# A fused attention and gated MLP kernel: two weight reads and the steps that follow them, put at other places in round 2

## The chip, the core and the metric

The kernel runs on one core of a Trainium2 chip. The metric is the time of one execution in device microseconds, the median of several runs. Lower is better.

## What is computed

Eight batches of 448 tokens go through an attention with 12 heads of 64 and a sigmoid in the softmax's place, and then through a gated MLP whose gate is mixed over the tokens:

```python
scores = q @ k.T / sqrt(64) - log(448)
x = concat_heads(sigmoid(scores) @ v)            # 8 x 448 x 768
h = relu(x @ w_in)                               # w_in: 768 x 1024
u, v = h[..., :512], h[..., 512:]
v_n = (v - mean(v)) / sqrt(var(v) + 1e-6)
v_s = w_spatial @ v_n + b_spatial[:, None]       # over tokens
out = (u * v_s) @ w_out                          # w_out: 512 x 768
```

Everything is float32. The large products are made from high and low parts of their operands: a copy rounded for TensorE (the high part) and the rest (the low part), with three products per pair.

## The kernel before, in words

**Rounds.** A round (`m`, 0 to 3; the text counts them 1 to 4) takes two batches through attention and then through the MLP. In rounds 2 to 4 the MLP's products follow Strassen's scheme: an operand is cut into four blocks, and seven products of blocks and of sums of blocks take the place of eight (`by_blocks`, operand names such as "11", "s2", "t3"). The weights need sums of blocks for that, and x needs such sums as well.

**Where the weights' sums come from.** In round 1 the joined values of w_in's two halves are written to DRAM, `w_full["g"]` for the gate half and `w_full["u"]` for the other. `weight_sums(kind, w)` (L522) is called twice at the start of round 2 (L1565, L1566). It issues one DMA that reads the whole values back into SBUF (L525, 1,536 KB), and appends a generator of eight steps to the list `jobs`. Steps 1 to 4 make one sum of blocks each on VectorE (L543, L546, L549, L552) and, one step later, ScalarE casts the sum to its high part (L535). Steps 5 to 8 are the finishing passes: VectorE subtracts the high part for the low one (L539), and SyncE writes both to DRAM (L540). From there `load_block` (L508) reads the blocks back for the products. `wholes(m)` (L579) is a third job: two steps that add x's high and low parts to whole values for the sums of x (L584).

**Who runs the jobs.** `spare(n)` (L478) takes n steps from the list, in its order, wherever it is called. The instructions of each engine run in the order in which the program issues them (`in_program_order`), and SyncE issues all DMAs of this stretch, so the place of a call in the code sets the place on every engine's queue.

**Attention by fours.** `attention_by_fours(m)` (L1311) takes the 12 units of a round (a unit is a batch and two heads) in three groups of four. For a group, `n` is its first unit. The loads of the next units' q and k (`raw`, L308) are issued at its start (L1337) and after its first splits (L1361). Then come 12 score tiles on TensorE (L378): VectorE copies four of them out of PSUM (L1354), ScalarE puts the others through the sigmoid (L342). VectorE splits the next units' operands into high and low parts (`attention_splits`, L321 and L328). The value products (L1382) fill two accumulators, `pavs[0]` and `pavs[1]`. After a part of them come `late` (a table of functions by group), `spare` and `split_values` (L131 on ScalarE, L132 on VectorE), which empties `pavs[0]`; `pavs[1]` is emptied by a copy on ScalarE (L1484 after the first group, L1480 after the second). The next group's short scores (L360, the tail of 64 tokens) and their sigmoids stand between.

**PSUM.** All of these tiles share one pool of four buffers of two banks (`ps_2`). They go round: the first score tile of a group takes the buffer of `pavs[0]`, the second that of `pavs[1]`, the third and fourth those of the two short tiles, the fifth that of the first.

The calls in question, at the end of a group that another one follows:

```python
for f in late.pop(n - first, ()):
    f()
spare(8 if n + 4 == end else 3 if n > first else 6)
...
    split_values(pavs[0], *units[n])
if n + 4 < end:
    spare(1)
```

So the two jobs of eight steps are run in pieces of 6 and 1 (first group), 3 and 1 (second group) and 8 (third group, with the two steps of `wholes`). After the last group `values_by_blocks` (L589) makes the sums of x (L628 and the lines behind it) and starts the gate products (`vx`, L1016).

Of the kernel before, what the change touches and what calls it, by code (L numbers as in the profile page):

```python
# [14 lines left out]
P = 128  # L15
# [20 lines left out]
def attn_gmlp_kernel(  # L36
# [485 lines left out]
    def weight_sums(kind, w):  # L522

        w7, order = KINDS[kind]
        nc.sync.dma_start(w[:, 1].bitcast(F32), w_full[kind])  # L525

        def both(name):
            at = NAMES.index(name) * BLOCK
            return w[:, :, at : at + BLOCK]

        def whole(name):
            return both(name)[:, 1].bitcast(F32)

        def cast(name):
            nc.scalar.copy(both(name)[:, 0], whole(name))  # L535

        def finish(name, of):
            hi, lo = (both(name)[:, a] for a in range(2))
            nc.vector.tensor_sub(lo, whole(name), hi.bitcast(F32))  # L539
            nc.sync.dma_start(w7[order.index(of)], both(name).bitcast(F32))  # L540

        def steps():
            nc.vector.tensor_add(whole("22"), whole("21"), whole("22"))  # L543
            yield True
            cast("22")
            nc.vector.tensor_sub(whole("21"), whole("11"), whole("21"))  # L546
            yield True
            cast("21")
            nc.vector.tensor_sub(whole("11"), whole("22"), whole("11"))  # L549
            yield True  # L550
            cast("11")
            nc.vector.tensor_sub(whole("12"), whole("12"), whole("11"))  # L552
            yield True
            cast("12")
            finish("22", "s1")
            yield True
            finish("21", "s3")
            yield True
            finish("11", "s2")
            yield True  # L560
            finish("12", "s4")
            yield True

        jobs.append(steps())

    def high_of_sum(name):
        nc.scalar.copy(staged[name][:, 0], whole[name])
# [726 lines left out]
    def ahead(f, n, end=len(units)):  # L1294
        if n < end:
            f(*units[n])

    def start_loads(m):
# [6 lines left out]
        if not m:  # L1305
            ahead(attention_loads, n + 3)

    late = {}
    early = {}

    def attention_by_fours(m):  # L1311
# [18 lines left out]
        for n in range(first, end, 4):  # L1330
# [4 lines left out]
                short_scores(n + 2)  # L1335
            for i in range(3):
                ahead(attention_loads, n + 4 + i, end)  # L1337
            ats, pending = {}, []
            for i, t in full:
                unit = units[n + i // 2 * 2]  # L1340
# [77 lines left out]
            if not m:  # L1418
                sigmoid(ats[by_vector[2]], ats[by_vector[2]])
                for pair in range(2):  # L1420
                    order = sorted(full[6 * pair : 6 * pair + 6], key=lambda at: at in by_vector)
                    for i, t in order:
                        value_products(
                            pavs[pair],
                            *units[n + 2 * pair],
                            t + i % 2 * (NFULL + 1),
                            ats[i, t],
                            start=i not in begun,
                        )
                        begun.add(i)  # L1430
                    if pair == 0:
                        last_scores()
                        load_weights(7 if n + 4 < end else 9)
                        for i2 in range(3):
                            ahead(attention_splits, n + 4 + i2, end)
                for pair in range(2):
                    unit = units[n + 2 * pair]
                    value_products(pavs[pair], *unit, NFULL, shorts[n + 2 * pair], start=False)
                split_values(pavs[0], *units[n])
                ahead(value_loads, n + 4, end)  # L1440
            else:
                one, two = firsts
                value_steps(0, one[:2])
                value_steps(1, two[:1])
                leave(0, value_steps(0, one[2:]))
                value_steps(1, two[1:2])
                leave(0, value_steps(0, one, swapped=True))
                last_scores()
                ahead(attention_splits, n + 6, end)
                for f in late.pop(n - first, ()):  # L1450
                    f()
                spare(8 if n + 4 == end else 3 if n > first else 6)
                value_steps(1, two[2:3])
                if n + 4 == end:
                    leave(1, value_steps(1, two[3:]))
                value_steps(0, [(NFULL, NFULL)])
                if n + 4 == end and m:
                    whole = whole_x["tile"]
                    x, odd = x_of(*units[n])[:, :, 1], pavs[0][:, 1, :S]
                    nc.scalar.copy(whole[:, 2, 2], pavs[0][:, 0, :S])  # L1460
                    nc.scalar.copy(x[:, 0], odd)
                    nc.vector.tensor_sub(whole[:, 3, 0], odd, whole[:, 2, 0])
                    nc.vector.tensor_sub(x[:, 1], odd, x[:, 0].bitcast(F32))
                else:
                    split_values(pavs[0], *units[n])
                if n + 4 < end:
                    spare(1)
                ahead(value_loads, n + 4, end)
                if n + 4 < end:
                    leave(1, value_steps(1, two[3:]))  # L1470
                    short_scores(n + 4)
                value_steps(1, firsts[1][1:], swapped=True)
# [71 lines left out]
    for m in range(B // 2):  # L1544
        ring = []
        if m:
            whole_x["tile"] = const.tile([P, 4, KH, S], F32, tag="w_out", name=f"whole_{m}")
            early.update(
                (i, whole_x["tile"][:, 2 + i].rearrange("p k s -> p (k s)")[:, : 2 * S])
                for i in range(2)  # L1550
            )

            def gate_ring():
                ring.append(gate_region(f"w_g7_{m}")[:, GAP : GAP + 8 * BLOCK])
                w_g.append(ring[0])
                for pos in range(HELD):
                    load_block("g", ORDER_1, pos)

            def up_ring(ps):
                for pos in ps:  # L1560
                    load_block("u", ORDER_V, pos)

            if m == 1:
                sums_of = gate_region("w_g_sums")[:, : 8 * BLOCK]
                weight_sums("g", sums_of.rearrange("p (a c) -> p a c", a=2))  # L1565
                weight_sums("u", const.tile([P, 2, NCC * F], F32R, tag="w_u", name="w_u_sums"))  # L1566
            else:
                w_u.append(const.tile([P, 2, NCC * F], F32R, tag="w_u", name=f"w_u_{m}"))
                late[0] = [lambda: up_ring(range(2))]
                late[4] = [lambda: up_ring(range(2, HELD))]  # L1570
            late[8] = [lambda: jobs.append(wholes(m)), gate_ring]
        attention(m)
        slots_of_mlp(m)
        b0, b1 = 2 * m, 2 * m + 1
# [92 lines left out]
```

## Time and profile before

| what | value |
|---|---|
| median of 3 runs | 641.74 us (640.69 to 644.13) |
| the profiled execution | 641.68 us |
| its span, first to last instruction | 638.8 us |
| TensorE busy with products | 624.8 us, 98% |
| VectorE busy | 453.8 us, 71% |
| ScalarE busy | 341.3 us, 53% |
| GpSimd busy | 20.8 us, 3% |
| mean granted clock of TensorE | 0.993 of full speed |
| HBM traffic over the span | 217 GB/s |

The span is 2.9 us shorter than the execution's time; this rest lies outside the instructions. Busy shares are means over stages with different limits. The chain of waits follows the execution back from its last instruction, at each step to what released it; what stands in it set the end.

### The profile page before, as it was taken

What the parts mean: (1) busy time and instruction counts of PE and PEld (TensorE: products, weight loads), DVE (VectorE), ACT (ScalarE), POOL (GpSimd) and SP (SyncE); (2) the same over time, 40 slices, a digit from 0 to 9 for tenths busy, and PEclk for the clock granted to TensorE, in tenths of its full rate; (3) what the DMA queues carried; (4) which work ended last, traced back from release to release, by engine and by line L of the source; (5) the groups of instructions that cost most, each with busy time, mean ns of one, the idle gap of its engine ahead of it and who ended that gap; (6) DMA issues with size and microseconds to landing.
All of it is one profiled execution on the core that took longest, in us unless ns stands there. A gap on an engine that the chain in (4) does not pass through costs nothing.

```text
span 638.8 us, 10383 instructions
## 1 busy us (share of the span) xinstructions
PE 624.8 (98%) x4136; PEld 488.4 (76%) x4136; DVE 453.8 (71%) x635; ACT 341.3 (53%) x444; POOL 20.8 (3%) x63
## 2 busy tenths in 40 slices
PE   9999999999978989999999999999999999999997
PEld 3646789999826649999985667999996655999996
DVE  4989789999758868277775757638788555835773
ACT  6987322345658853173457785137247776516443
POOL 0000001000000000010000000002000000002000
PEclk9999999999998999999999999999999999999999
DMA  8774754279948768691575662487169554559044
GB/s 298 266 228 143 225 149 140 71 308 355 342 180 324 294 257 327 175 392 70 191 266 211 242 246 97 123 284 310 33 225 350 196 184 169 168 135 392 30 152 169
DMA packets 59632, 139.22 MB, mean 218 GB/s; under 512 B 15680, under 2 KB 31552, under 8 KB 59328
## 3 DMA queue, kind: packets, MB, share of 16 engines
q1 hardware_dynamic: 59152, 138.22, 61.9%
q8 instruction: 32, 0.52, 0.3%
q10 hardware_dynamic: 432, 0.34, 0.2%
q14 instruction: 16, 0.13, 0.1%
HBM read 102.37 MB, written 36.18 MB: 217 GB/s over the span
## 4 chain that ended last, share of the span: by engine, by line
PE 91%; DVE 3%; DMA 3%; ACT 1%; issue 1%; SPq 0%; ACTq 0%; DVEq 0%
PE o L1016 16%; PE psc L378 13%; PE pav L1382 12%; PE pg L950 10%; PE vx L1016 7%; PE ux L1016 7%; PE uy L1016 5%; PE pav L427 5%; PE pv L460 5%; PE pu L460 5%; PE vy L1016 3%; DMA raw<-qk_dram 3%; PE psc L360 3%; ACT xs L619 1%; PE pg L925 1%
## 5 line engine op out<-in xcount | busy, mean ns | idle before, releaser
L342 ACT ACTIVATE ats<-psc,bias_s 128x896 f32<-128x896 f32 x102 | 95.2, 1008 | 22.2 <-PE pav L1382 13.5
L378 PE MATMUL psc<-qks 64*128 64x448 f32 x840 | 90.0, 369 | 6.0 <-DVE x_s L132 6.0
L378 PEld LDWEIGHTS psc<-qks 64*128 64x128 f32 x840 | 79.1, 188 | 21.0 <-DVE x_s L132 7.7
L1382 PE MATMUL pav<-ats,v 64*64 64x448 f32 x720 | 76.0, 539 | 0.0
L1016 PE MATMUL o<-x_s,w_out 128*128 128x448 f32 x324 | 65.8, 362 | 0.0
L950 PE MATMUL pg<-w_sp_s,mlp 128*128 128x448 f32 x320 | 65.8, 364 | 0.0
L1016 PEld LDWEIGHTS o<-x_s,w_out 128*128 128x128 f32 x324 | 60.6, 188 | 4.3
L950 PEld LDWEIGHTS pg<-w_sp_s,mlp 128*128 128x128 f32 x320 | 59.7, 188 | 5.2 <-issue 1.2
L1382 PEld LDWEIGHTS pav<-ats,v 64*64 64x64 f32 x720 | 28.2, 132 | 37.4 <-issue 26.3
L328 DVE TENSOR_TENSOR qks<-raw,qks 128x848 fp32r<-128x848 f32 x46 | 47.4, 1040 | 1.1
L1016 PE MATMUL vx<-x_s,w_g 128*128 128x448 f32 x216 | 45.3, 365 | 2.6 <-ACT vr L676 2.5
L1016 PEld LDWEIGHTS vx<-x_s,w_g 128*128 128x128 f32 x216 | 40.0, 188 | 8.4 <-ACT vr L676 3.7
L1016 PE MATMUL ux<-x_s,w_u 128*128 128x448 f32 x162 | 33.9, 362 | 0.0
L1016 PEld LDWEIGHTS ux<-x_s,w_u 128*128 128x128 f32 x162 | 30.4, 188 | 2.0
L321 DVE CAST qks<-raw 128x848 fp32r<-128x848 f32 x38 | 22.7, 597 | 10.1 <-DMA raw<-qk_dram 7.9
L460 PE MATMUL pu<-x_s,w_u_s 128*128 128x448 f32 x144 | 29.0, 362 | 0.0
L460 PE MATMUL pv<-w_g_s,x_s 128*128 128x512 f32 x126 | 28.9, 391 | 0.0
L460 PEld LDWEIGHTS pu<-x_s,w_u_s 128*128 128x128 f32 x144 | 27.0, 188 | 1.8
L460 PEld LDWEIGHTS pv<-w_g_s,x_s 128*128 128x128 f32 x126 | 23.6, 188 | 5.6 <-PE pav L427 0.7
L1085 ACT CAST x_s<-g 128x896 fp32r<-128x896 f32 x11 | 10.4, 944 | 32.1 <-DVE g L1082 32.1
L427 PE MATMUL pav<-ats,v 128*64 128x448 f32 (+1 forms) x144 | 27.1, 545 | 0.0
L1170 DVE TENSOR_TENSOR us<-uy,us 128x448 f32<-128x448 f32 x6 | 3.7, 621 | 32.6 <-ACT us L1169 32.6
(205 smaller groups left out, 1022.9 us busy)
## 6 DMA issues: line engine op xcount, KB each, us to landing
raw<-qk_dram SPq DMA_DIRECT2D x47, 456.0 KB, 6.1
w_g<-w_g SPq DMA_DIRECT2D x21, 768.0 KB, 6.8
w_u<-w_u SPq DMA_DIRECT2D x21, 768.0 KB, 6.7
w_out<-w_out SPq DMA_DIRECT2D x21, 768.0 KB, 10.0
v<-v_dram SPq DMA_DIRECT2D x24, 448.0 KB, 4.3
wraw<-w_in_dram SPq DMA_DIRECT2D x12, 512.0 KB, 5.0
v<-vt SPq DMA_DIRECT2D x48, 112.0 KB, 2.5
wraw<-w_out_dram SPq DMA_DIRECT2D x6, 512.0 KB, 4.2
```

What stands on the lines that cost most here:

```text
L321: (nc.vector.tensor_copy if b > 1 or halfway else nc.scalar.copy)(s[:, 0], raw)
L328: nc.vector.tensor_sub(s[:, 1], loaded[b, hp][:, HALF:], s[:, 0].bitcast(F32))
L342: nc.scalar.activation(at, src, AF.Sigmoid, bias=bias_s, scale=QK)
L360: nc.tensor.matmul(psc[odd * HALF : (odd + 1) * HALF, j, :S], raw[rows, :HALF], raw[rows, HALF + Q :], start=True, stop=True,)
L378: nc.tensor.matmul(psc[:, j, :S], st[rows, k : k + P], mv[rows, Q:PART], start=i == 0, stop=i == len(ops) - 1,)
L427: nc.tensor.matmul(pav[heads, odd, :S], vt[rows, t, heads], at[rows, j], start=start, stop=t == NFULL,)
L460: nc.tensor.matmul(ps, st, mv, start=i == 0, stop=i == len(ops) - 1)
L619: nc.scalar.copy(t[:, 0], src[:, ks])
L950: nc.tensor.matmul(pg[:, i, :S], st, mv, start=n == 0 and not ended, stop=n == len(ops) - 1 and ended,)
L1016: nc.tensor.matmul(out_ps, stationary(w, i, k)[:, a], moving[mv][k][c], start=(to, i) not in started and n == 0, stop=n == len(ops) - 1, s ...
L1085: nc.scalar.copy(homes[name][0][:, i], src[:, i])
L1382: ins = nc.tensor.matmul(pavs[pair][heads, i % 2, :S], vt[rows, t if t == NFULL else t + i % 2 * (NFULL + 1), heads], at[rows, j], start=i ...
```

## The change

`weight_sums` no longer issues its DMA itself but returns a function that does. For w_g that function is put into a new table, `soon`, and is called in the first group of round 2 behind the three unit loads at the group's start; for w_u it goes into `late` and is called after the splits of that group, behind the fourth unit load. The pieces of the jobs become 5 and 2 in the first group and 4 and 2 in the second, where they were 6 and 1, and 3 and 1; so 13 of the 16 steps, and no longer 11, stand ahead of the third group. There, `wholes` is put at the head of the list, ahead of the steps that are left of w_u's. The other rounds have no other job in the list at that point.

```diff
@@ -522,7 +522,9 @@
     def weight_sums(kind, w):
 
         w7, order = KINDS[kind]
-        nc.sync.dma_start(w[:, 1].bitcast(F32), w_full[kind])
+
+        def load():
+            nc.sync.dma_start(w[:, 1].bitcast(F32), w_full[kind])
 
         def both(name):
             at = NAMES.index(name) * BLOCK
@@ -562,6 +564,7 @@
             yield True
 
         jobs.append(steps())
+        return load
 
     def high_of_sum(name):
         nc.scalar.copy(staged[name][:, 0], whole[name])
@@ -1305,6 +1308,7 @@
         if not m:
             ahead(attention_loads, n + 3)
 
+    soon = {}
     late = {}
     early = {}
 
@@ -1335,6 +1339,8 @@
                 short_scores(n + 2)
             for i in range(3):
                 ahead(attention_loads, n + 4 + i, end)
+            for f in soon.pop(n - first, ()):
+                f()
             ats, pending = {}, []
             for i, t in full:
                 unit = units[n + i // 2 * 2]
@@ -1449,7 +1455,7 @@
                 ahead(attention_splits, n + 6, end)
                 for f in late.pop(n - first, ()):
                     f()
-                spare(8 if n + 4 == end else 3 if n > first else 6)
+                spare(8 if n + 4 == end else 4 if n > first else 5)
                 value_steps(1, two[2:3])
                 if n + 4 == end:
                     leave(1, value_steps(1, two[3:]))
@@ -1464,7 +1470,7 @@
                 else:
                     split_values(pavs[0], *units[n])
                 if n + 4 < end:
-                    spare(1)
+                    spare(2)
                 ahead(value_loads, n + 4, end)
                 if n + 4 < end:
                     leave(1, value_steps(1, two[3:]))
@@ -1562,13 +1568,14 @@
 
             if m == 1:
                 sums_of = gate_region("w_g_sums")[:, : 8 * BLOCK]
-                weight_sums("g", sums_of.rearrange("p (a c) -> p a c", a=2))
-                weight_sums("u", const.tile([P, 2, NCC * F], F32R, tag="w_u", name="w_u_sums"))
+                soon[0] = [weight_sums("g", sums_of.rearrange("p (a c) -> p a c", a=2))]
+                sums_of = const.tile([P, 2, NCC * F], F32R, tag="w_u", name="w_u_sums")
+                late[0] = [weight_sums("u", sums_of)]
             else:
                 w_u.append(const.tile([P, 2, NCC * F], F32R, tag="w_u", name=f"w_u_{m}"))
                 late[0] = [lambda: up_ring(range(2))]
                 late[4] = [lambda: up_ring(range(2, HELD))]
-            late[8] = [lambda: jobs.append(wholes(m)), gate_ring]
+            late[8] = [lambda: jobs.insert(0, wholes(m)), gate_ring]
         attention(m)
         slots_of_mlp(m)
         b0, b1 = 2 * m, 2 * m + 1
```

SyncE's queue at the start of round 2, before (`v` and `raw` are loads of a unit's values and of its q and k, the first number in a name is the head pair):

```order
L313 DMA v_2_1488<-v_dram 128x896
L525 DMA w_g_sums<-w_full_g 128x3072
L525 DMA w_u_sums<-w_full_u 128x3072
L308 DMA raw_4_1508<-qk_dram 128x912
L308 DMA raw_5_1510<-qk_dram 128x912
L308 DMA raw_0_1512<-qk_dram 128x912
L308 DMA raw_1_1550<-qk_dram 128x912
L540 DMA w_g<-w_g_sums 256x1x768 x3
L313 DMA v_4_1689<-v_dram 128x896
L313 DMA v_0_1715<-v_dram 128x896
L308 DMA raw_2_1726<-qk_dram 128x912
```

and with the change:

```order
L313 DMA v_2_1488<-v_dram 128x896
L308 DMA raw_4_1506<-qk_dram 128x912
L308 DMA raw_5_1508<-qk_dram 128x912
L308 DMA raw_0_1510<-qk_dram 128x912
L527 DMA w_g_sums<-w_full_g 128x3072
L308 DMA raw_1_1549<-qk_dram 128x912
L527 DMA w_u_sums<-w_full_u 128x3072
L542 DMA w_g<-w_g_sums 256x1x768 x3
L313 DMA v_4_1689<-v_dram 128x896
L313 DMA v_0_1715<-v_dram 128x896
L308 DMA raw_2_1726<-qk_dram 128x912
```

The three loads ahead of L308's fourth now precede both weight reads, and w_u's read follows the fourth load; from the writes of w_g's results on the order is as it was.

VectorE between the first and the second group, from the sums of w_g to the copy of the second group's first score tile, before:

```order
L543 TENSOR_TENSOR w_g_sums<-w_g_sums 128x768
L546 TENSOR_TENSOR w_g_sums<-w_g_sums 128x768
L549 TENSOR_TENSOR w_g_sums<-w_g_sums 128x768
L552 TENSOR_TENSOR w_g_sums<-w_g_sums 128x768
L539 TENSOR_TENSOR w_g_sums<-w_g_sums 128x768 x2
L132 TENSOR_TENSOR x_s<-pav_0_1624,x_s 128x2x448
L539 TENSOR_TENSOR w_g_sums<-w_g_sums 128x768
L1485 CAST x_s<-ats_1495 128x2x448
L1354 COPY wval_s<-psc_4_0_1732 128x896
```

and with the change:

```order
L545 TENSOR_TENSOR w_g_sums<-w_g_sums 128x768
L548 TENSOR_TENSOR w_g_sums<-w_g_sums 128x768
L551 TENSOR_TENSOR w_g_sums<-w_g_sums 128x768
L554 TENSOR_TENSOR w_g_sums<-w_g_sums 128x768
L541 TENSOR_TENSOR w_g_sums<-w_g_sums 128x768
L132 TENSOR_TENSOR x_s<-pav_0_1623,x_s 128x2x448
L541 TENSOR_TENSOR w_g_sums<-w_g_sums 128x768 x2
L1491 CAST x_s<-ats_1493 128x2x448
L1360 COPY wval_s<-psc_4_0_1732 128x896
```

One finishing pass has gone from ahead of L132, which empties the first accumulator, to behind it, where there are now two.

VectorE at the same place between the second and third group, before:

```order
L539 TENSOR_TENSOR w_g_sums<-w_g_sums 128x768
L543 TENSOR_TENSOR w_u_sums<-w_u_sums 128x768
L546 TENSOR_TENSOR w_u_sums<-w_u_sums 128x768
L132 TENSOR_TENSOR x_s<-pav_0_1843,x_s 128x2x448
L549 TENSOR_TENSOR w_u_sums<-w_u_sums 128x768
L1354 COPY wval_s<-psc_2_0_1937 128x896
```

and with the change:

```order
L541 TENSOR_TENSOR w_g_sums<-w_g_sums 128x768
L545 TENSOR_TENSOR w_u_sums<-w_u_sums 128x768
L548 TENSOR_TENSOR w_u_sums<-w_u_sums 128x768
L551 TENSOR_TENSOR w_u_sums<-w_u_sums 128x768
L132 TENSOR_TENSOR x_s<-pav_0_1843,x_s 128x2x448
L554 TENSOR_TENSOR w_u_sums<-w_u_sums 128x768
L541 TENSOR_TENSOR w_u_sums<-w_u_sums 128x768
L1360 COPY wval_s<-psc_2_0_1942 128x896
```

ScalarE there, before:

```order
L535 CAST w_u_sums<-w_u_sums 128x768
L131 CAST x_s<-pav_0_1843 128x2x448
L535 CAST w_u_sums<-w_u_sums 128x768
L342 ACTIVATE at_2_3_1908<-psc_2_3_1909,bias_s 128x2x448
L1480 COPY whole_1490<-pav_1_1844 128x896
L342 ACTIVATE at_4_3_1930<-psc_4_3_1931,bias_s 128x2x448
L342 ACTIVATE ats_1495<-psc_2_1_1945,bias_s 128x896
```

and with the change:

```order
L537 CAST w_u_sums<-w_u_sums 128x768 x2
L131 CAST x_s<-pav_0_1843 128x2x448
L537 CAST w_u_sums<-w_u_sums 128x768 x2
L342 ACTIVATE at_2_3_1913<-psc_2_3_1914,bias_s 128x2x448
L1486 COPY whole_1490<-pav_1_1844 128x896
L342 ACTIVATE at_4_3_1935<-psc_4_3_1936,bias_s 128x2x448
L342 ACTIVATE ats_1493<-psc_2_1_1950,bias_s 128x896
```

A third sum of w_u stands ahead of L132 on VectorE, the fourth sum and a finishing pass behind it; on ScalarE two casts instead of one stand ahead of L131 and two instead of one behind it, ahead of the short scores' sigmoid and of the copy that empties the second accumulator.

## Rows read from the trace of the kernel before

**Rows 1.** Chain of waits, rounds 2 and 3: start us, us, what.

```profile
166.14 1.73 PE psc L360 x16
...
168.79 13.05 DMA raw<-qk_dram
...
231.23 3.02 DVE whole L584 x2
...
239.04 3.88 PE vx L1016 x18
...
328.86 1.80 PE psc L360 x16
...
350.28 7.42 PE psc L378 x72
...
377.31 10.75 PE pav L1382 x112
...
388.08 1.10 DVE whole L628
...
391.91 3.87 PE vx L1016 x18
```

**Rows 2.** Timeline of TensorE: start us, us, instruction, [idle before <-releaser].

```profile
193.41 9.00 PE L378 MATMUL psc<-qks 64*128 64x448 f32 x72 [5.99 <-DVE x_s L132]
...
239.04 1.28 PE L1016 MATMUL vx<-x_s,w_g 128*128 128x448 f32 x5 [2.47 <-ACT vr L676]
```

**Rows 3.** Timeline of SyncE's queue, round 2: DMA issues.

```profile
167.81 0.41 SPq L525 DMA_DIRECT2D w_g_sums<-w_full_g  x1
168.28 0.42 SPq L525 DMA_DIRECT2D w_u_sums<-w_full_u  x1
...
168.79 4.09 SPq L308 DMA_DIRECT2D raw<-qk_dram  x4
...
191.46 3.35 SPq L540 DMA_DIRECT2D w_g<-w_g_sums  x3
```

**Rows 4.** DMA issues, by kind: count, KB each, us from issue to landing.

```profile
w_g_sums<-w_full_g SPq DMA_DIRECT2D x1, 1536.0 KB, 9.2
...
raw<-qk_dram SPq DMA_DIRECT2D x1, 456.0 KB, 12.6
```

**Rows 5.** Windows: busy us of each engine, granted clock, DMA share, GB/s.

```profile
176.00:182.00 6.00, 6.00 (x71) 2.55 (x67) 0.14 (x1) 4.43 (x5) 0.20 (x2) 1.00 0.99 412
...
190.00:192.00 2.00, 0.00 (x0) 0.00 (x0) 2.00 (x3) 1.84 (x3) 0.00 (x0) 0.50 0.00 0
...
238.00:240.00 2.00, 0.96 (x5) 0.90 (x6) 1.97 (x3) 1.43 (x4) 0.00 (x0) 1.00 0.96 375
```

**Rows 6.** Timeline of VectorE and ScalarE between the first and second group of round 2.

```profile
181.86 0.60 DVE L321 CAST qks<-raw 128x848 fp32r<-128x848 f32 x1 [6.70 <-DMA raw<-qk_dram]
...
186.63 0.95 DVE L543 TENSOR_TENSOR w_g_sums<-w_g_sums 128x768 f32<-128x768 f32 x1
...
191.34 0.90 ACT L131 CAST x_s<-pav 128x896 fp32r<-128x896 f32 x1
...
192.27 1.09 DVE L132 TENSOR_TENSOR x_s<-pav,x_s 128x896 fp32r<-128x896 f32 x1
...
193.28 0.95 DVE L539 TENSOR_TENSOR w_g_sums<-w_g_sums 128x768 fp32r<-128x768 f32 x1
```

**Rows 7.** Timeline of VectorE and ScalarE between the second and third group of round 2.

```profile
204.13 0.60 DVE L321 CAST qks<-raw 128x848 fp32r<-128x848 f32 x1 [1.24 <-DMA raw<-qk_dram]
...
207.94 1.04 DVE L328 TENSOR_TENSOR qks<-raw,qks 128x848 fp32r<-128x848 f32 x1
...
212.28 0.83 ACT L535 CAST w_u_sums<-w_u_sums 128x768 fp32r<-128x768 f32 x1
...
213.02 1.01 ACT L342 ACTIVATE at<-psc,bias_s 128x896 f32<-128x896 f32 x1
...
213.92 0.91 ACT L1480 COPY whole<-pav 128x896 f32<-128x896 f32 x1
```

## Prediction

> **What bounds the kernel now.** I began with the busy shares: TensorE is busy for 98% of the span, so only its gaps can be won, or time at a lower clock. Then I compared the rounds in the chain of waits. Round 2 runs from its first score products at 166.14 us to 239.04, where the gate products' second operand starts: 72.9 us. Round 3 does the same work from 328.86 to 391.91, 63.05 us [rows 1]. So round 2 has about 9.8 us that its neighbour hasn't.
>
> The timeline of TensorE says where. It stands still for 5.99 us before 193.41, and the 72 score products then take 9.00 us [rows 2] instead of 7.42 [rows 1], 1.58 more: the granted clock is 0.50, its lower level of 1.2 GHz, from the idle stretch on [rows 5]. At the end of the round it waits 2.47 us more before 239.04 [rows 2]. That makes 10.0 us; the rest of the round is 0.2 us quicker than round 3.
>
> The cause is upstream. SyncE issues w_g's and w_u's whole values at 167.81 and 168.28 and the next units' loads only then [rows 3]. The first of these is 13.05 us on its way [rows 1]; VectorE has sat idle for 6.70 us when it lands at 181.84 [rows 6]. Three splits later, at 186.63, the sums of w_g start; L132, which frees the first bank that TensorE wants, stands behind them and runs from 192.27, and TensorE goes on at 193.41 [rows 2, 6]. At the round's end the whole values of x (L584) run at 231.23 [rows 1], behind w_u's finishing passes; in round 3 the step that follows (L628) starts 0.02 us after the last value product, at 377.31 + 10.75 = 388.06 [rows 1].
>
> **The loads.** The queue keeps its bytes, and its order changes: three unit loads of 456 KB go ahead of w_g's 1,536 KB, the fourth stands between w_g and w_u. At the 412 GB/s of this stretch [rows 5] the first load loses 3.1 MB in front of it, 7.6 us, and lands at 174.2, before VectorE wants it (181.86 - 6.70 = 175.16) [rows 6]. w_g landed at 167.81 + 9.2 = 177.0 [rows 3, 4]; 1.40 MB ahead of it cost 3.4 us: 180.4. VectorE's three splits end at 175.16 + 3 x 1.6 = 180.0. So the sums start at **T = 180.4** instead of 186.63. The fourth load and w_u wait on nothing new: the fourth keeps its wait for a buffer, and the queue has drained by about 172.44 + 12.6 = 185.0 in either order [rows 4], long before w_u's sums are begun.
>
> **First to second group.** From T to TensorE's start I take 193.41 - 186.63 = 6.78 us as it is [rows 2, 6]: L131 on ScalarE, which stands behind the four casts of w_g there, ends at 192.24 and sets L132's 192.27 [rows 6], so one finishing pass fewer ahead of L132 gives nothing. T + 6.78 = 187.2, and TensorE is free at 193.41 - 5.99 = 187.42. The gap goes, and with it the fall of the clock. Two finishing passes of 0.95 us instead of one [rows 6] now stand between L132 and the copy that frees the bank for the fifth score tile: some 0.6 us for TensorE, which the next part covers.
>
> **What is late next.** The third write of w_g's results is issued when the last of these passes ends: T + (192.27 + 1.09 - 186.63) + 2 x 0.93 = T + 8.6 = 189.0, where it was 193.28 + 0.95 = 194.23 [rows 6]. Behind it SyncE's queue holds two value loads and then the loads of the third group's units, the first of which VectorE got at 204.13, after waiting 1.24 us for it [rows 7]. From the last pass to that landing it was 9.9 us with the engines full; the bytes ahead are the same, so it lands at 198.9. VectorE would be ready at 195.9: before it was 204.13 - 1.24 = 202.89, 9.5 us after TensorE's start, of which 1.58 were the slow clock, and I add the 0.6. **The DMA queue sets this group**, though TensorE's own work would let it go on at 187.4 + 0.6 + 19.6 = 207.6 (350.28 back to 328.86, less the first 1.80 us of shorts [rows 1], is 19.6 per group).
>
> **Second to third group.** Three splits end 208.98 - 204.13 = 4.85 us after the landing [rows 7], at S = 203.75. Now three steps of w_u instead of two stand ahead of L132, and two instead of one behind it, with two casts on ScalarE. From S on: the last pass of w_g and three sums of about 0.95 us each (S + 3.75); ScalarE's second cast ends at S + 3.6, L131 takes 0.90 and L132 1.09: S + 5.5, and TensorE may start. Then the fourth sum to S + 6.4, and the fourth cast, which waits for it, 0.83 to S + 7.25. Behind that cast on ScalarE stand the sigmoid of the short scores (1.01, S + 8.2) and the copy of the second accumulator, L1480 (0.91) [durations from rows 6, 7]. That copy frees the bank of the second score tile: **S + 9.0 = 212.75**. Before, L1480 ended at 213.92 + 0.91 = 214.83 [rows 7], before TensorE needed it. The new wait is about 3 us long; VectorE's own extra pass ends at S + 7.25 and is covered by it. From below this wait can cost nothing, if S comes early; the bound above is these 3 us and what S slips.
>
> The write of w_u's first result now stands ahead of the third group's two value loads on SyncE's queue, issued at S + 7.25 = 211.0. Those values are wanted at 219.5. The third write of w_g, with two such loads and one more load behind, took 9.9 us in all; one write less should bring them in time, and the worst is some 1.4 us, kept for the range.
>
> **The end of the round.** Eleven score tiles of 7.42 / 12 us, 10.75 us of value products and the 3.85 us from 388.06 to 391.91 [rows 1] follow: 212.75 + 6.8 + 10.75 + 3.85 = 234.15. The whole values run straight behind VectorE's last copies, ahead of the three finishing passes that are left, and both end more than 4 us before the last product: the 2.47 us go. w_u's blocks are read back no later than before. Nothing changes on PE or POOL, nor in the other rounds, where the list of jobs is otherwise empty.
>
> **Sum.** 239.04 - 234.15 = 4.9 us of the 9.8 are won: 6.0 + 1.6 + 2.5 at the three places, less some 5 at the two waits that come instead. The profiled execution took 641.68 us, 0.06 below the median of the runs shown: 641.7 - 4.9 = **636.8 us**. What can be told from no change is about 0.5%, 3.2 us: below 638.5 is faster, above 644.9 slower.
>
> **The rivals.**
> - *All comes back.* If the third group's loads land when VectorE is ready, S = 195.9 + 4.85 = 200.75, 3.0 us sooner: 633.8. If ScalarE's copy isn't waited for either, round 2 ends as round 3 does, 391.91 - 350.28 = 41.63 us after 187.4, at 229.0: 631.7. For it speaks that the second group's neighbour in round 3 has no such wait; against it, that VectorE waited 1.24 us already with a TensorE at half clock [rows 5, 7]. Chance 0.20.
> - *The clock falls at the new wait.* The gap of 5.99 us brought the granted clock to 0.50, that of 2.47 left it at 1.00 [rows 2, 5]; 3 us lie between, nearer to the second. If it falls, the third group's scores take the 9.00 us once more: 636.8 + 1.6 = 638.4. Chance 0.10. [...]
> - *w_g's values come too late.* If the DMA engines shared their time among the reads under way, w_g's would end with w_u's, at 185.0 or later. The end of the round is T + 53.75, so from T = 185.3 on nothing is won; at the old 186.63 the second pass behind L132 makes it 1.35 us worse: 643.0, slower than before. Against it: the small load behind the two big ones landed 4.8 us after w_g did (181.84 against 177.0), in the order of issue [rows 1, 4]. Chance 0.03. The Trainium skill (DMA: Bandwidth & Descriptors, Queues, rings and completion order) says that each engine takes the descriptors of one queue in ring order, though completion is not strictly first in, first out; by that rule this rival is out.
> - *Part of it.* T or the third group's loads slip by 1.7 us to 4.9 us, through the value loads or a slower drain: 638.5 to 641.7. Chance 0.12.
>
> **How the numbers follow.** The forecast has the remaining 0.55, its own range 635.2 to 638.4. 8 times in 10 the time should lie between 633.6 and 639.4: this leaves out the full return to 631.7 (0.05), most of the partial case (0.10) and the late values (0.03). Faster by over 0.5%: 0.54 + 0.20 + half of the clock's 0.10 and a little of the partial case, 0.81. Same: 0.17. Slower: 0.02.
>
> **What would show it.** Right: no idle of TensorE before the second group and its scores in about 8 us at full clock; w_g landing near 180.4; VectorE waiting for the third group's first load; a wait of some 3 us before the second score tile of the third group, released by L1480's copy; no wait at the second gate operand beyond round 3's. It is wrong if TensorE still stands over 1 us before the second group (T was late), or if the third group begins without a wait (the queue was sooner than I say).

## The result and the profile after

The changed kernel takes 635.89 us (median of 6 runs, 635.44 to 636.25), the kernel before 641.93 us (6 runs). The ratio is 0.990, 95% interval 0.987 to 0.993: 6.0 us faster, where 4.9 was forecast. In the profiled executions the span falls from 638.8 to 634.0 us, by 4.8, and the time from 641.68 to 635.77, by 5.9: the other microsecond lies outside the instructions, 2.9 us before and 1.8 with the change. One execution is not the median. The spans of the kernel before, in its runs beside the experiments below, lie between 637.3 and 642.4 us, and in the eleven profiles that follow round 2 starts anywhere from 165.43 to 166.91 us, ahead of every edit. So a single profile places a wait well and a total only to within some 2 us.

The chain of waits of the changed kernel, round 2 (start us, us, what):

```profile
165.77 1.67 PE psc L360 x16
...
168.97 10.92 DMA w_g_sums<-w_full_g
...
191.50 6.24 DMA raw<-qk_dram
...
210.84 1.67 PE psc L378 x12
...
212.55 7.26 PE psc L378 x48
219.81 10.76 PE pav L1388 x112
...
230.59 1.10 DVE whole L631
...
234.42 3.87 PE vx L1019 x18
```

The round starts at 165.77 and reaches the gate products' second operand at 234.42: 68.65 us, where it was 72.9 before and 63.05 in round 3 [rows 1]. So 4.25 us of the 9.8 came back and some 5.6 are still there. Of the 4.8 us of span, 0.37 stand ahead of round 2, where nothing was changed. The chain runs through w_g's read, then through the third group's first load at 191.50, then through the start of the third group.

TensorE's timeline shows the rest (start us, us, instruction, [idle before <-releaser]):

```profile
187.01 2.68 PE L378 MATMUL psc<-qks 64*128 64x448 f32 x24
189.97 5.08 PE L378 MATMUL psc<-qks 64*128 64x448 f32 x48 [0.28 <-DVE wval_s L1360]
195.63 1.74 PE L1388 MATMUL pav<-ats,v 64*64 64x448 f32 x16 [0.58 <-ACT wval_s L342]
...
208.20 0.88 PE L378 MATMUL psc<-qks 64*128 64x448 f32 x6 [0.32 <-DVE x_s L132]
210.84 8.97 PE L378 MATMUL psc<-qks 64*128 64x448 f32 x66 [1.76 <-ACT at L342]
```

The idle stretch of 5.99 us ahead of the second group [rows 2] is gone: its scores start at 187.01 without a wait. Two small waits follow, 0.28 and 0.58 us. The third group is where the time is lost now: its first score tile starts at 208.20, its second only at 210.84 after 1.76 us of idle, and the rest of its scores take 8.97 us instead of about 6.8. The windows say why these are slow (busy us of each engine, granted clock, DMA share, GB/s):

```profile
208.00:210.00 2.00, 0.88 (x6) 0.48 (x6) 2.00 (x4) 0.95 (x2) 0.00 (x0) 1.00 0.00 0
...
214.00:216.00 2.00, 2.00 (x14) 1.76 (x14) 1.99 (x2) 1.16 (x2) 0.00 (x0) 0.50 1.03 416
```

The clock is at 1.00 while TensorE waits and at 0.50, its lower level, for a while behind it. VectorE's timeline answers to [rows 6] and [rows 7]:

```profile
174.72 0.59 DVE L321 CAST qks<-raw 128x848 fp32r<-128x848 f32 x1
...
179.91 0.96 DVE L545 TENSOR_TENSOR w_g_sums<-w_g_sums 128x768 f32<-128x768 f32 x1 [0.34 <-DMA w_g_sums<-w_full_g]
...
185.55 1.09 DVE L132 TENSOR_TENSOR x_s<-pav,x_s 128x896 fp32r<-128x896 f32 x1 [0.84 <-ACT x_s L131]
186.56 1.82 DVE L541 TENSOR_TENSOR w_g_sums<-w_g_sums 128x768 fp32r<-128x768 f32 x2
...
197.76 0.60 DVE L321 CAST qks<-raw 128x848 fp32r<-128x848 f32 x1 [2.20 <-DMA raw<-qk_dram]
...
201.58 1.04 DVE L328 TENSOR_TENSOR qks<-raw,qks 128x848 fp32r<-128x848 f32 x1
...
208.07 0.95 DVE L554 TENSOR_TENSOR w_u_sums<-w_u_sums 128x768 f32<-128x768 f32 x1
...
219.66 3.02 DVE L587 TENSOR_TENSOR whole<-x_s 128x1344 f32<-128x1344 f32 x2
222.59 2.69 DVE L541 TENSOR_TENSOR w_u_sums<-w_u_sums 128x768 fp32r<-128x768 f32 x3
...
230.59 1.09 DVE L631 TENSOR_TENSOR whole<-pav,whole 128x896 f32<-128x896 f32 x1
```

VectorE no longer waits for the next units' load: the splits start at 174.72, straight behind the last copy. It waits 0.34 us for w_g (179.91) and 2.20 us for the third group's first load (197.76). From there it works without a gap to L132 but for ScalarE's casts. x's whole values (L587) run at 219.66, and L631 starts with the last value product; the 2.47 us of idle at the round's end are gone. ScalarE at the boundary to the third group:

```profile
209.05 0.83 ACT L537 CAST w_u_sums<-w_u_sums 128x768 fp32r<-128x768 f32 x1 [1.29 <-DVE w_u_sums L554]
209.79 1.00 ACT L342 ACTIVATE at<-psc,bias_s 128x896 f32<-128x896 f32 x1
210.69 0.90 ACT L1486 COPY whole<-pav 128x896 f32<-128x896 f32 x1
211.47 1.02 ACT L342 ACTIVATE at<-psc,bias_s 128x896 f32<-128x896 f32 x1
```

The cast at 209.05 has waited 1.29 us for w_u's fourth sum on VectorE (L554, 208.07). The short scores' sigmoid stands behind it and ends at 210.79; TensorE goes on at 210.84. The loads of weights for the second, third and fourth score tile (PEld) name what each of them waited for:

```profile
210.84 0.50 PEld L378 LDWEIGHTS psc<-qks 64*128 64x128 f32 x6 [2.13 <-ACT at L342]
211.64 0.50 PEld L378 LDWEIGHTS psc<-qks 64*128 64x128 f32 x6 [0.30 <-ACT whole L1486]
212.55 3.68 PEld L378 LDWEIGHTS psc<-qks 64*128 64x128 f32 x22 [0.41 <-ACT at L342]
```

### The profile page after: what moved, and what is told of

Its sections match the earlier page's. It is cut to its first block, busy times and chain, and to the rows that moved or that the text cites. A ratio compares the mean times of both kernels' runs of the same rounds, so it can differ in the third digit from the quotient of the medians.

```text
span 634.0 us, 10384 instructions
## 1 busy us (share of the span) xinstructions
PE 625.6 (99%) x4136; PEld 488.2 (77%) x4136; DVE 453.7 (72%) x635; ACT 341.6 (54%) x444; POOL 21.0 (3%) x63
## 4 chain that ended last, share of the span: by engine, by line
PE 91%; DVE 3%; DMA 3%; ACT 2%; issue 1%; SPq 0%; ACTq 0%; DVEq 0%
PE o L1019 16%; PE psc L378 13%; PE pav L1388 12%; PE pg L953 10%; PE vx L1019 7%; PE ux L1019 7%; PE uy L1019 5%; PE pav L427 5%; PE pu L460 5%; PE pv L460 5%; PE vy L1019 3%; PE psc L360 2%; DMA w_g_sums<-w_full_g 2%; DMA raw<-qk_dram 1%; PE pg L928 1%
## 5 line engine op out<-in xcount | busy, mean ns | idle before, releaser
L1388 PEld LDWEIGHTS pav<-ats,v 64*64 64x64 f32 x720 | 28.7, 132 | 37.6 <-issue 26.0
L1388 PE MATMUL pav<-at,v 64*64 64x448 f32 x168 | 27.0, 536 | 0.0
```

The lines of the kernel that those rows point to most:

```text
L1388: ins = nc.tensor.matmul(pavs[pair][heads, i % 2, :S], vt[rows, t if t == NFULL else t + i % 2 * (NFULL + 1), heads], at[rows, j], start=i ...
```

## The experiments

Ten kernels ran, and the changed one once more. Times are medians, of four executions in most cases, with the ratio to the kernel before on the same chip and its 95% interval; "round 2" is the stretch from the first score products to the gate's second operand in the profile. Seven of the kernels took 0.3 to 2.6 us longer than the highest time that was expected of them; the lengths of round 2 came nearer, within 1.0 us. Where the rest went is open. Both reads were moved together in every kernel with the new loads, so what each of the two is worth is not known.

**The loads alone.** The changed kernel with the old pieces and the whole values last:

```diff
-                spare(8 if n + 4 == end else 4 if n > first else 5)
+                spare(8 if n + 4 == end else 3 if n > first else 6)
-                    spare(2)
+                    spare(1)
-            late[8] = [lambda: jobs.insert(0, wholes(m)), gate_ring]
+            late[8] = [lambda: jobs.append(wholes(m)), gate_ring]
```

> The two weight reads stand where the change put them; the pieces of the jobs are those of before (6 and 1, 3 and 1, 8) and x's whole values come last again. Theory (the order of the loads gives the gain, the moved steps take part of it back at the third group, the early whole values give 2.5 us): the sums of w_g start near 179.9 us as in the changed kernel, no idle before the second group; the third group begins without the wait of 2 us for ScalarE's copy and at full clock; 2.5 us of idle come back before the second gate operand. Round 2 takes 66.0 us (72.9 before, 68.65 changed), the time is about 633.3, 2.6 under the changed kernel. Rival (the pieces 5, 2, 4 and 2 are what makes the third group possible at all): slower than the changed kernel by the 2.5 us of the whole values, 638.4.

Measured: 634.6 us, 0.989 (0.986 to 0.993), and round 2 took 65.85 us. The place of the two reads gives the whole gain, and a little more than the full change. TensorE began the third group without a wait, though VectorE waited as long for that group's first load as in the changed kernel:

```profile
197.69 0.60 DVE L321 CAST qks<-raw 128x848 fp32r<-128x848 f32 x1 [2.31 <-DMA raw<-qk_dram]
```

So with the old pieces this wait costs TensorE nothing. The time missed the 633.3 because the idle of 2.47 us, which left the clock alone in the kernel before [rows 2, 5], brought it down here; the 18 products took 5.46 us instead of 3.88:

```profile
232.05 5.46 PE L1019 MATMUL vx<-x_s,w_g 128*128 128x448 f32 x18 [2.47 <-ACT vr L679]
```

and in the window behind the idle the granted clock is 0.55:

```profile
232.00:234.00 2.00, 1.95 (x6) 1.74 (x7) 1.97 (x2) 0.43 (x1) 0.00 (x0) 0.55 1.02 409
```

One of the four executions kept a mean clock of 0.999, against 0.996 or 0.997 in the others, and it took 633.52 us.

**The whole values alone.** The kernel before with `jobs.insert(0, wholes(m))`.

> The kernel before, with x's whole values at the head of the list in the third group and nothing else. Theory: the 2.47 us of idle before the second gate operand go and nothing else moves; round 2 takes 70.5 us, the time is 2.4 us under before's. Rival (w_u's late finishing passes then hold VectorE in the values' place): no change, 0 to 0.5 us.

Measured: 639.54 us, 0.996 (0.994 to 0.998), 2.5 us faster; round 2 took 70.4 us. The theory holds. A wait of 0.89 us for a block of w_g came up later in the gate products, which returns below.

**The pieces alone.** The kernel before with the pieces 5 and 2, 4 and 2.

> The kernel before, with the pieces 5, 2, 4 and 2 and nothing else: both weight reads still stand ahead of the units' loads, the whole values come last. Theory: the first idle of 6 us stays, the wait for ScalarE's copy in the third group comes as in the changed kernel (3.7 us later than before, 5.3 if the clock falls), and the 2.5 us at the round's end go because w_u's steps are nearly done: round 2 takes 74.2 to 75.8 us, 1 to 3 us slower than before. Rival (more steps ahead of the third group help by themselves): 2.4 us faster than before.

Measured: 642.34 us, 1.001 (0.999 to 1.002). In the profile round 2 took 75.1 us, 2.2 longer, as expected:

```profile
193.66 9.62 PE L378 MATMUL psc<-qks 64*128 64x448 f32 x72 [6.03 <-DVE x_s L132]
...
218.27 8.51 PE L378 MATMUL psc<-qks 64*128 64x448 f32 x66 [1.75 <-ACT at L342]
```

Both waits are there, the old one of 6.03 us and the new one of 1.75 us. The median shows nothing of the 2.2 us: the theory's cost is seen in the trace, its size in the time isn't (1 to 3 us slower was expected; the median is 0.3 slower, and the interval goes from 0.4 us quicker to 1.5 slower). That the pieces help by themselves is out.

**One step behind L132.** The changed kernel, second group only:

```diff
-                    spare(2)
+                    spare(1 if n > first else 2)
```

> The changed kernel, but one step instead of two behind L132's place between the second and third group (the fourth sum of w_u; its fourth cast and first finishing pass go to the third group). Theory (the fourth cast, which waits for the fourth sum and stands on ScalarE ahead of the copy that empties the second accumulator, makes TensorE wait, and the wait brings the clock down): the second score tile of the third group starts near 209.6 us instead of 212.55 and the clock stays at full speed, 2.9 and 1.6 us less: round 2 takes 64.1 us, the time is about 631.4. Rival (the landing of the third group's first load and VectorE's passes set the place, not the cast): 0.9 us less at most, 635.

Measured: 633.76 us, 0.987 (0.984 to 0.990), 2.1 us under the changed kernel's median; round 2 took 65.1 us and the clock stayed up. The 212.55 in the expectation was misread: it is the fourth tile's start, the second's is 210.84. Without the fourth cast the short scores' sigmoid starts at 208.33, right behind the third, and the 72 scores run through:

```profile
207.59 0.83 ACT L537 CAST w_u_sums<-w_u_sums 128x768 fp32r<-128x768 f32 x1
208.33 1.01 ACT L342 ACTIVATE at<-psc,bias_s 128x896 f32<-128x896 f32 x1
...
208.87 7.94 PE L378 MATMUL psc<-qks 64*128 64x448 f32 x72 [0.66 <-DVE x_s L132]
...
242.99 7.45 PE L1019 MATMUL vx<-x_s,w_g 128*128 128x448 f32 x36 [0.50 <-DMA w_g<-w_g]
```

So the cast made the wait, and in this profile the slow clock went with it. The time is still 2.4 us above the 631.4 expected, and round 2 is 1.0 us longer than said. The last line is new and was in no expectation: TensorE waits 0.50 us for w_g's fifth block. SyncE issues its load at 233.04, behind w_u's reads and 1.6 us after the gate's second operand starts; in the changed kernel it is issued 0.04 us before that.

**The fourth sum ahead of L132.** The changed kernel with `spare(8 if n + 4 == end else 5)` and `spare(1 if n > first else 2)`.

> The changed kernel with the pieces 5 and 1 in the second group instead of 4 and 2: the fourth sum of w_u moves from behind L132 to ahead of it, all else stays, the number of steps too. Theory (the copy of the second accumulator is late because the fourth cast, ahead of it on ScalarE, waits for a sum that stands behind L132 on VectorE): the first score tile of the third group starts 1.0 us later than in the changed kernel, the second 1.8 us earlier; with a shorter gap the clock stays up. Round 2 takes 65.3 us, or 66.9 if the clock falls; the time is 632.5 to 634.1. Rival (the count of steps ahead of the third group sets the wait): as the changed kernel or 1 us slower, 635.9 to 636.9.

Measured: 635.15 us, 0.989 (0.988 to 0.991), 0.7 us under the changed kernel; round 2 took 67.7 us. The wait moved to the first tile and was 2.01 us long, the second tile followed at once, and in the profile the clock fell again, to 0.50 in the window below:

```profile
202.00 0.60 DVE L321 CAST qks<-raw 128x848 fp32r<-128x848 f32 x1 [0.54 <-DMA raw<-qk_dram]
...
210.25 9.20 PE L378 MATMUL psc<-qks 64*128 64x448 f32 x72 [2.01 <-DVE x_s L132]
```

```profile
212.00:214.00 2.00, 2.00 (x14) 1.73 (x14) 0.87 (x2) 2.00 (x3) 0.00 (x0) 0.50 0.88 299
```

So it is the cast behind L132, not the count of steps, that holds the second tile; but the sum costs about as much where it delays L132. The first tile came 1.5 us later than in the changed kernel, counted from the start of the round, where 1.0 was expected: the other 0.5 us is VectorE's wait of 0.54 us for that group's third load (202.00), which the changed kernel's first profile doesn't have. The time, 635.15, lies between the theory's 634.1 and the rival's 635.9 and decides nothing. In the other three executions the mean clock was 0.999 or 1.0, and they took 634.75 to 635.19 us, so the clock's fall is not what keeps this kernel from the expected time.

**w_g's writes behind the loads.** The changed kernel with other pieces:

```diff
-                spare(8 if n + 4 == end else 4 if n > first else 5)
+                spare(8 if n + 4 == end else 3 if n > first else 5)
-                    spare(2)
+                    spare(2 if n > first else 0)
```

> The changed kernel with the pieces 5 and 0 in the first group and 3 and 2 in the second: three of w_g's finishing passes, and with them their writes, now stand behind the loads of the third group's units on SyncE's queue, and ScalarE has one cast of w_u, not four, near the boundary to the third group. Theory (these writes and the value loads behind them are what the third group's first load waits for, and ScalarE's casts are the other wait): VectorE no longer waits for that load (2.2 us in the changed kernel), TensorE idles nowhere before the gate products, round 2 takes 63.0 to 63.5 us (68.65 changed, 63.05 in round 3). Then w_u is finished late and w_g's fifth block, queued behind w_u's blocks, may come up to 1 us late: the time is 630.5 to 631.5. Rival (the chip's DMA engines are simply full in this stretch, in whatever order): VectorE still waits 1 us or more for that load and round 2 takes 65 us or more.

Measured: 633.88 us, 0.988 (0.985 to 0.990); round 2 took 63.5 us. Only one write of w_g stands ahead of the third group's loads on SyncE's queue, and they are issued at 187.54 instead of 191.50:

```profile
185.30 0.53 SPq L542 DMA_DIRECT2D w_g<-w_g_sums  x1
...
187.54 5.00 SPq L308 DMA_DIRECT2D raw<-qk_dram  x4
```

From issue to landing the first of them took 5.8 us, 6.2 in the changed kernel; so it is the issue that came sooner. VectorE goes from its last copy (194.25) to the splits without a wait, and TensorE through the third group without one:

```profile
194.25 1.09 DVE L1360 COPY ats<-psc 128x896 f32<-128x896 f32 x1
195.26 0.59 DVE L321 CAST qks<-raw 128x848 fp32r<-128x848 f32 x1
...
207.02 7.74 PE L378 MATMUL psc<-qks 64*128 64x448 f32 x72
...
242.72 7.45 PE L1019 MATMUL vx<-x_s,w_g 128*128 128x448 f32 x36 [1.93 <-DMA w_g<-w_g]
```

That settles VectorE's wait for the load: it was late because it stood behind w_g's writes on SyncE's queue, not because the DMA engines had no room in whatever order. Round 2 is as short as expected, but the time is 2.4 us above the 631.5. The gate products now wait 1.93 us for w_g's fifth block. SyncE issues w_u's four reads ahead of it, and these wait for w_u's last write.

**w_u's reads one place later.** As the last one; `up_ring(range(HELD))` is called in `then` behind the first reload of w_g's ring.

```diff
                 spare(i)
+                if i and up_late:
+                    up_late.pop()()
...
-            up_ring(range(HELD))
+            up_late.append(lambda: up_ring(range(HELD)))
```

> As the kernel with the pieces 5 and 0, 3 and 2, and w_u's four blocks are read back behind the reload of w_g's first ring place (the fifth block) instead of ahead of it. Theory (SyncE's queue holds w_g's fifth block behind w_u's reads, which wait for w_u's last writes): no wait for w_g's blocks is left in the gate products; 630.2, the fastest of all, and 0.3 to 1.3 us under the same kernel without this. Rival (that wait is not the queue's order but the engines' load): no difference between the two.

Measured: 632.75 us, 0.985 (0.984 to 0.987). In the profiles the span is 631.2 us against 631.3, and the wait only moved: w_g's sixth block was 12.45 us on its way and TensorE waited 1.81 us for it, one product on. The medians are 1.1 us apart, as expected (0.3 to 1.3), and all four executions are quicker than the four without the edit. This profile is the longest of its four and the other the shortest of its own, so the pair doesn't show where the 1.1 us come from.

```profile
229.38 0.33 SPq L508 DMA_DIRECT2D w_g<-w_g  x1
231.11 1.77 SPq L508 DMA_DIRECT2D w_u<-w_u  x4
233.66 3.92 SPq L508 DMA_DIRECT2D w_g<-w_g  x2
```

The reload of the sixth block is issued at 233.66, right behind w_u's 3.1 MB. The expectation that no wait would be left was wrong, and 630.2 us was not reached: the bytes ahead of a block delay it as well as what SyncE waits for.

**The old pieces, the loads, the whole values first and w_u's reads one place later.**

> The changed loads and x's whole values first, the pieces of before (6 and 1, 3 and 1), and w_u's blocks read back behind w_g's fifth. Theory: as the kernel with the loads alone, without its 2.47 us of idle before the gate products and the 1.6 us of low clock behind it: round 2 takes 63.4 us, the time is 630.6. Rival (the pieces of the change are needed for w_u to be ready): a wait for a block of w_g or w_u of 1 us or more in the gate products, 632 or more.

Measured: 632.67 us, 0.984 (0.982 to 0.987); round 2 took 64.1 us, and no block was waited for, so the rival's wait is out, though the time is what the rival gave (632 or more). Round 2 is 0.7 us longer than expected; that stands at the second group, where w_g's read landed later (11.44 us after its issue) and the value load was 0.77 us late:

```profile
188.45 7.49 PE L378 MATMUL psc<-qks 64*128 64x448 f32 x72 [0.23 <-DVE x_s L132]
196.71 1.73 PE L1391 MATMUL pav<-ats,v 64*64 64x448 f32 x16 [0.77 <-DMA v<-v_dram]
```

The other 1.4 us of the miss in time are not in round 2; the round starts at 166.91 here, 1.1 us later than in the changed kernel's profile, ahead of every edit.

**w_u's reads last.** Pieces 5 and 0, 3 and 2, with w_u's reads behind all three reloads of w_g, once behind the first four writes of the turned gate values and once ahead of them. The lines are those of the second kernel; in the first, the call stands behind `turn(0, 0, r1)` for two of the blocks and in the next branch for the other two:

```diff
                 if i:
+                    if up_late:
+                        up_ring(up_late.pop(0))
                     turn(0, 0, r1)
```

> As the kernel with the pieces 5 and 0, 3 and 2, but w_u's four blocks are read back behind all three reloads of w_g's ring and behind the first four writes of the turned gate values. Theory (w_u's reads ahead of a ring block delay it, by SyncE's wait or by the bytes in front): TensorE waits for no block of w_g (1.93 and 1.81 us in the two kernels before this) and none of w_u; the mixing over tokens starts 47.4 us after the gate's second operand, as in round 3; the time is 1.9 us under the kernel with those pieces alone, 631.0 to 632.0. Rival (the turned values then come late): a wait of 1 us or more before the mixing over tokens.

> The same, with w_u's reads behind the three reloads of w_g's ring but ahead of all writes of the turned gate values. Theory: the same time as the kernel with the reads behind four of those writes, within 0.5 us, for the turned values are wanted some 25 us later. Rival: the 3.1 MB ahead of them bring a wait before the mixing over tokens.

Measured: 632.32 us, 0.985 (0.981 to 0.988), behind those writes: no wait for w_g, but one of 0.60 us for w_u. Ahead of them: **631.35 us, 0.984 (0.980 to 0.987)**, the lowest median of all, 11.0 us under the 642.40 of before on this chip and 4.5 under the changed kernel. The two medians are 1.0 us apart where at most 0.5 was expected, but the times of their executions overlap, so which place is better is not shown. The chain of the second:

```profile
229.89 3.87 PE vx L1021 x18
...
277.25 4.01 PE pg L955 x20
```

From the gate's second operand to the mixing over tokens it takes 47.36 us, as in round 3, with no wait in between, and round 2 takes 63.5 us, within 0.5 of round 3. The rival, a wait of 1 us or more before the mixing, showed in neither.

**The changed kernel again**, on the chip of the last two.

> The changed kernel again, on the chip of the two runs beside it, to compare directly: 635.9 us as before, and 4 us over the kernels beside it. Its wait of some 2 us in the third group of round 2 again, and the clock at half behind it in this profile too if the fall belongs to the wait and not to chance.

Measured: 635.83 us, 0.991 (0.987 to 0.994); the same wait, and the clock at 0.50 behind it again:

```profile
209.52 0.87 PE L378 MATMUL psc<-qks 64*128 64x448 f32 x6 [0.71 <-DVE x_s L132]
212.15 8.23 PE L378 MATMUL psc<-qks 64*128 64x448 f32 x66 [1.76 <-ACT at L342]
```

## Why the prediction was right

The forecast was 636.8 us, within 633.6 to 639.4, with 0.81 on faster by over 0.5%. Measured were 635.9 and 0.94% of gain. The path through the loads, the queue and the cast was right; two terms at the third group were wrong and nearly cancelled, and that part of the hit is luck. Step by step, in us from the start of the round (forecast, measured; 166.14 and 165.77 are the starts):

| step | forecast | measured |
|---|---|---|
| w_g's sums start (T) | 14.3 | 14.1 |
| TensorE starts the second group | 21.3 | 21.2 |
| last finishing pass behind L132 ends | 22.9 | 22.6 |
| third group's first load is split | 32.8 | 32.0 |
| splits end (S) | 37.6 | 36.9 |
| third group's first score tile | 43.1 | 42.4 |
| its second score tile | 46.6 | 45.1 |
| value products start | 53.4 | 54.0 |
| the gate's second operand | 68.0 | 68.7 |

*The loads.* Right, to 0.2 us. The read of w_g, issued behind three unit loads, took 10.92 us. Counted from the start of the round it landed 3.3 us later than before (14.1 against 10.9), and the 1.40 MB that had come in front of it are 3.4 us at 412 GB/s. So the bytes in front set the landing, in the order of issue. The order agrees with the ring order of the Trainium skill (DMA: Bandwidth & Descriptors, Queues, rings and completion order).

*First to second group.* Right. The small wait behind the two passes was 0.28 us, not 0.6; another 0.58 us at the value products, for a sigmoid, was not foreseen. Both were covered by the load that followed, as forecast.

*What is late next.* Right in kind: VectorE waited 2.20 us. The load came 0.8 us sooner than the 9.9 us from the last pass said (197.76 - 188.38 = 9.4, and the pass itself was 0.25 sooner). The kernel with the writes behind the loads shows that the queue's order was the cause. By itself this wait costs TensorE nothing: the kernel with the loads alone has it too (2.31 us), and there TensorE doesn't stop. It counts only together with the steps that the change put behind it.

*Second to third group.* The step that failed is "That copy frees the bank of the second score tile: S + 9.0". TensorE went on at 210.84, 0.05 us after the short scores' sigmoid (210.79) and ahead of the end of L1486 (211.59). S + 8.2 was the forecast's own time for that sigmoid, and 202.62 + 8.2 = 210.8 is what came. The third tile waited for L1486 and the fourth for the second short sigmoid, by their loads of weights. So the four buffers came free for the next tiles in the order in which the program empties them (L132, the short sigmoid, L1486, the second short sigmoid), and the second score tile takes the first short tile's place, not the second accumulator's; the description ahead of the forecast has the two the wrong way round. The wait was 1.76 us, not about 3. The cast that waits for w_u's fourth sum was the cause, as the kernel without it showed.

*The clock.* It had a chance of 0.10 as a rival, and it fell, in two profiles of the changed kernel. A wait of 1.76 us, with 0.32 and 0.71 us of idle shortly before, went ahead of the fall, though 2.47 us had left it alone in the kernel before. Weighing the new wait between the gaps of 2.47 and 5.99 us by its length was the second step that failed. The rest of the scores took 8.97 us instead of 6.8, 2.2 more, but the second tile had started 1.5 us sooner than said: 0.8 by the load, 0.8 by the order of the buffers. These are errors of opposite sign, and by luck they leave 0.6 us.

*The end of the round.* Right: the 2.47 us went, L631 starts 0.02 us after the last value product (219.81 + 10.76 = 230.57), and the whole values alone are worth 2.5 us.

*What the parts are worth.* Alone, the loads gave 7.4 us, the whole values 2.5, the pieces nothing that can be measured. Together they gave 6.0. By that difference (7.4 + 2.5 - 6.0) the pieces cost some 4 us once the loads are in place; this is an estimate, for no kernel has the loads, the whole values first and the old pieces alone. The nearest, which also moves w_u's reads, is 3.2 us under the changed kernel. In the trace the cost stands at the third group. Counted from the start of the round, its first score tile came 1.3 us later than with the loads alone, for the third sum ahead of L132 and a load that was 0.5 us later; then came the 1.76 us for the cast, and the slow clock. The kernel that has neither sum nor cast at that place, nor the wait for the load, has round 2 at 63.5 us. But finishing w_u earlier has a use that the forecast didn't see: when it is finished late, w_u's reads hold up w_g's ring on SyncE's queue, by 0.5 to 1.9 us.

## What to carry to other kernels

In this kernel one engine issues all transfers, and a large read with a late use cost what it delayed, not what it took: put such a read behind the small loads that the next step needs, and look what the writes of its results are then queued ahead of. A step that is moved into another engine's slack brings its casts and its DMAs with it; look for the neighbour in the same queue that has to wait for the step, not at the step's own length (0.95 us for the sum here, 1.76 us for TensorE). When a wait goes, follow each queue to the next place where it runs empty; here the time came back there, at the third group and at w_g's blocks.

## What had not been expected of the hardware

The clock's fall is not a matter of one gap's length. The 2.47 us of idle ahead of the gate's second operand left it at 1.00 in the kernel before and brought it down in the kernel with the loads alone, with the same instructions around it. Gaps of 1.75, 1.76 and 2.01 us at the third group were followed by the lower level in four profiles. The same kernel doesn't do it every time. In one of the changed kernel's timed runs (632.9 us of span, the shortest of its six) the mean clock was 1.00, in the others 0.996 or 0.997; in the kernel with the fourth sum ahead of L132 it was 0.997 in the profiled execution and 0.999 or 1.0 in the three others. What decides it is open; no run here tells.
